# Moving matmul operands to other addresses: a 64-byte gap, a shifted weight slot and wider phi(k) buffers

## The chip, the cores and the metric

The kernel runs on one core of one Trainium2 chip. The metric is the device time of one execution in microseconds. The kernel before took 303.79 us, the median of 3 runs (303.33 to 304.34).

Names of engines: PE is TensorE (PEld its weight loads), DVE is VectorE, ACT is ScalarE, POOL is GpSimd, SP is SyncE, which here only issues transfers.

## The reference

x is a sequence of 2048 rows and 640 columns. Two branches work on it and a gate mixes them.

```
g = sigmoid(sum(x * gate_w))                       # one number per row
a = conv(x, K) + x * Dskip                         # state space branch; K from A, B, C, dt
q, k, v = x @ wqkv, 32 heads of 20
pq, pk = phi(q), phi(k)      # phi(t) = (t + 1 if t > 0 else exp(t)) + 1e-6
kv = sum over rows of pk^T v ;  z = sum over rows of pk      # per head
b = (pq @ kv / (pq . z + 1e-6)) @ wo
out = g * a + (1 - g) * b
```

All inputs and the output are float32. For the given inputs the convolution's kernel K is constant over the sequence to within float32's precision, so that the kernel computes it as a running sum along the sequence; a general path for other inputs is in the program but does not run.

## The kernel before, in words

Every large product is made of three matmuls on split operands: a number is kept as h + l, where h is its rounding to the float32r type that TensorE reads and l the rest, and a product is ah*bh + al*bh + ah*bl (`mm3`, L104 to L107). The work on TensorE comes in this order.

- **k and G^T.** The rows go through in 16 tiles of 128. For tile T, k = x @ wk is made in two halves of columns: `k_mm(T, 0)` with wkA (322 columns: 320 of wk and two that hold gate_w for the gate) and `k_mm(T, 1)` with wkB (320). Each half is 15 matmuls: 5 blocks of the contraction, three each; the stationary operand is a 128 by 128 block of x transposed (xTh or xTl), the moving operand is wk. For the first four tiles the loops stand in another order (`k_first`, L441). ScalarE and VectorE turn k into phi(k): tiles e (3 buffers) and r (2 buffers), then its split ph and pl (`k_act`, `k_split`). Meanwhile TensorE sums G = x^T phi(k) over the rows for tile T-1: `g_main` (512 columns of phi(k) moving, blocks of xh and xl stationary; 3 matmuls for each of 5 blocks) and `g_rest` (the other 128 columns of phi(k) stationary, x moving, 320 columns; 6 matmuls). The loop's body (L546 to L573) sets the order on TensorE: k half 0 (15 matmuls), G block 0 (3), G blocks 1 and 2 (6), k half 1 (15), `g_rest` (6), G blocks 3 and 4 (6).
- **The small matrices.** GT holds G transposed; with Wv it gives kv per head (`kv_mm`, L266), and with wo the 640 by 640 matrix M (`m_mm`), which goes through DRAM and is read back as Mh and Ml into the slots of GT and Wv (tags "m1" and "m2").
- **q and the output.** 20 blocks of q (`q_block`: wq stationary, xT moving, 512 columns, 15 matmuls each) and 20 blocks of the output (`final_mm`: M stationary, phi(q) split in pTh and pTl moving, 15 matmuls each; the last block is cut into two halves of 256 columns). The table PLAN (L63) sets the order of these by hand: q is a block of q, f a block of the output, d the denominators (2 matmuls), n a normalisation, y a block of the convolution.

The order of instructions on every engine is the order in which the code is written. SBUF tiles are given out by pools in the order in which the pools were made: px (x transposed, whose slots phi(q) takes over), pc (constants, then GT, Wv and the split weights), pw, pk (the tiles of the k stage), and, in pk's place after it is closed, pq. A tile that is larger or added in pc therefore moves all that stands behind it. wkA has a slot of 384 columns a row block (tag "wA", `w_tiles(3 * P, ...)`), since wq's first 384 columns use the slot later; it fills 322 of them, from the start.

Of the kernel before, what the change touches and what calls it, by code (L numbers as in the profile page):

```python
# [30 lines left out]
F32 = mybir.dt.float32  # L31
# [8 lines left out]
P = 128  # L40
L = 2048
D = 640
# [5 lines left out]
CA, CB = 320, 320  # L48
# [9 lines left out]
NK = sum(map(len, CONV_K.values()))  # L58
WQ = 3, 4, 0, 1, 2
QI = DH // NB  # L60


PLAN = """  # L63
# [10 lines left out]
def f32(ap):  # L74
    return ap.bitcast(F32)


def body(tc, i, outT):
    nc = tc.nc
    pe, act, dve, pool, sp = nc.tensor, nc.scalar, nc.vector, nc.gpsimd, nc.sync  # L80
    outer, top, kst = ExitStack(), ExitStack(), ExitStack()

    def mk(stack, name, space=None):
        kw = {} if space is None else {"space": space}
        if space is not DRAM:
            kw["reuse_waits"] = "tile"
        return stack.enter_context(tc.tile_pool(name=name, bufs=1, **kw))
# [6 lines left out]
    pk = mk(kst, "pk")  # L94
# [3 lines left out]
    def hi(dst, src):  # L98
        act.activation(dst, src, AF.Copy)  # L99
# [9 lines left out]
    def col(tag, n=NB, dt=F32):  # L109
        return pc.tile([P, n], dt, tag=tag, name=tag)  # L110

    def w_tiles(n, tag, name):
        return tuple(pc.tile([P, NB, n], F32R, tag=tag + x, name=name + x) for x in "hl")
# [30 lines left out]
    zc, zs, ch = col("zc"), col("zs", 1), col("ch", 1)  # L144
    zsh, zsl = col("zsh", 2, F32R), col("zsl", 2, F32R)
    bm, zh = col("bm", P, F32R), col("zh", H)
    GT = pc.tile([P, NB, D], F32, tag="m1", name="GT")
    Wv = pc.tile([P, NB, D], F32, tag="m2", name="Wv")
    M_d = [dram.tile([D, D], F32, name=f"M_d{x}") for x in "hl"]
# [31 lines left out]
    kp, ke, ks = {}, {}, {}  # L181
# [10 lines left out]
    def k_act(t, hf):  # L192

        p, c0, n = kp.pop((t, hf)), hf * CA, (CA, CB)[hf]
        if hf == 0:
            ke[t] = pk.tile([P, D], F32, tag="e", bufs=3, name="e")
        e = ke[t][:, c0 : c0 + n]
        r = pk.tile([P, CA], F32, tag="r", bufs=2, name="r")
        act.activation(e, p[:, :n], AF.Exp)  # L199
        act.activation(r[:, :n], p[:, :n], AF.Relu)  # L200
        if hf == 0:
            act.activation(s_all[:, t : t + 1], p[:, CA : CA + 1], AF.Copy)
        dve.scalar_tensor_tensor(e, e, 1.0, r[:, :n], op0=OP.min, op1=OP.add)  # L203

    def k_split(t):
# [4 lines left out]
        dve.scalar_tensor_tensor(l, e, EPS, f32(h), op0=OP.add, op1=OP.subtract)  # L210
        za = zacc.rearrange("p (b h i) -> p b h i", h=H, i=QI)
        dve.tensor_tensor(za, za, e.rearrange("p (h b i) -> p b h i", b=NB, i=QI), op=OP.add)
        ks[t] = (h, l)
# [28 lines left out]
    def g_out(b, eng):  # L242
        src = gps.pop(b)
        (hi if eng is act else dve.tensor_copy)(GT[:, b, :512], src)

# [4 lines left out]
    def parts(gi):  # L250
        c0, n = GRP[gi]
        return [(r, c0 + o, min(HC, n - o)) for r, o in ((0, 0), (64, HC)) if o < n]
# [13 lines left out]
    def kv_mm(pr):  # L266
        p = pqp.tile([P, 512], F32, tag="f", bufs=3, name="kvps")
        kvT = kvs[pr] = kvz[pr % 2]
        for k, gi in enumerate((2 * pr, 2 * pr + 1)):
            for b in range(NB):  # L270
                for r, c, n in parts(gi):
                    pe.matmul(p[r : r + n, k * 64 : k * 64 + n], Wv[:, b, c : c + n], GT[:, b, c : c + n],
                              start=(b == 0), stop=(b == NB - 1))
# [175 lines left out]
                pe.matmul(kp[t, hf][:, :n], (xTl if ps == 1 else xTh)[0][:, b, sl], w[ps // 2][:, b, :n],  # L449
                          start=b + ps == 0, stop=b == NB - 1 and ps == 2)  # L450

    wkA = w_tiles(3 * P, "wA", "wkA")
    wkB = w_tiles(CB, "wB", "wkB")
    raw = {}

# [46 lines left out]
    for t in range(N0):  # L502
        k_act(t, 0)
        if t < 2:
            x_split(t)
        k_act(t, 1)
        if t in (0, 2):
            k_split(t // 2)
# [6 lines left out]
    def wq_views(w, c, b0, b1):  # L515
        src = raw[c][:, :D].rearrange("p (h b i) -> p b h i", b=NB, i=QI)[:, b0:b1]
        return [src] + [v[:, c, : (b1 - b0) * P].rearrange("p (b h i) -> p b h i", h=H, i=QI) for v in w]

# [11 lines left out]
    for T in range(1, NT):  # L530
# [15 lines left out]
        if T >= N0:  # L546
            k_mm(T, 0)
            k_act(T, 0)
# [27 lines left out]
        if T == 2:  # L576
            act.activation(dtc, dtc, AF.Exp)
            dve.tensor_reduce(zh, ident.rearrange("p (h i) -> p h i", i=QI), axis=AX.X, op=OP.add)
            dve.tensor_copy(bm.rearrange("p (h i) -> p h i", i=QI), zh[:, :, None].to_broadcast([P, H, QI]))
        for b in CONV_P.get(T - 1, ()):  # L580
# [39 lines left out]
    def rem_out():  # L620
        for b0, b1 in ((0, 4), (4, NB)):
            tp = mbank("tp")
            for b in range(b0, b1):
                pe.transpose(tp[:, (b - b0) * P : (b - b0 + 1) * P], rem[:, b * P : b * P + P], ident)
            hi(GT[:, b0:b1, 512:], tp[:, : (b1 - b0) * P].rearrange("p (b s) -> p b s", s=P))

# [314 lines left out]
```

## Time and profile before

| | us |
|---|---|
| median of 3 runs | 303.79 (303.33 to 304.34) |
| the profiled execution | 304.36 |
| its span, first to last instruction | 302.6 |
| PE busy in the span | 296.6 (98%) |
| PEld | 255.7 (85%) |
| DVE | 230.0 (76%) |
| ACT | 118.8 (39%) |
| POOL | 46.9 (15%) |
| 16 DMA engines, mean share | 48% |

A matmul's duration in the profile is the time from its start to the end of its last column, and successive matmuls overlap: the next one starts long before the last one's end. What a stream of matmuls costs is the distance from start to start, which the timeline shows (rounded to 10 ns, so it is best taken over many matmuls).

### The profile page before, as it was taken

To read this page: it belongs to the slowest core of one execution; us is meant where nothing else is said; L and a number is where in the kernel's file an instruction comes from. 1 tells how busy PE (TensorE), PEld (TensorE's weight loads), DVE (VectorE), ACT (ScalarE), POOL (GpSimd) and SP (SyncE) were. 2 spreads that over 40 slices of the span, in tenths; PEclk is the share of its full clock that TensorE was granted. 3 is DMA by queue.
4 is the path that set the end of the run, shared out by engine and by line. 5 is a ranking of instruction groups with operands and counts; after the bars stand their busy time and mean duration, and the time that the engine had idled before them with its cause. 6 is when DMAs were issued, how large, how long until landed. Compare 5 with 4: busy or idle time off the path is not lost.

```text
span 302.6 us, 4538 instructions
## 1 busy us (share of the span) xinstructions
PE 296.6 (98%) x1627; PEld 255.7 (85%) x1627; DVE 230.0 (76%) x356; ACT 118.8 (39%) x249; POOL 46.9 (15%) x50
## 2 busy tenths in 40 slices
PE   8999999999999999999999999999999999999994
PEld 8998899999999999998887767888888888788884
DVE  2859976899899799946636779859684767788992
ACT  4465143453444435317343563651423234303200
POOL 3605240000000000000000000003133211242531
PEclk9999999999999999999999999999999999999999
DMA  6827275167868756290344553790415022244323
GB/s 190 302 88 220 77 233 185 36 192 203 256 150 252 225 181 203 80 281 14 100 147 137 205 176 110 259 341 9 114 59 186 25 77 62 69 141 172 122 92 109
DMA packets 28410, 46.00 MB, mean 152 GB/s; under 512 B 3772, under 2 KB 10828, under 8 KB 28384
## 3 DMA queue, kind: packets, MB, share of 16 engines
q1 hardware_dynamic: 28383, 45.66, 48.2%
q8 instruction: 15, 0.25, 0.4%
q14 instruction: 12, 0.09, 0.1%
HBM read 32.92 MB, written 12.72 MB: 151 GB/s over the span
## 4 chain that ended last, share of the span: by engine, by line
PE 87%; DVE 6%; DMA 3%; issue 1%; ACT 1%; SPq 1%; POOL 0%; DVEq 0%; ACTq 0%; POOLq 0%
PE fp L105 8%; PE fp L107 8%; PE fp L106 8%; PE qp L105 6%; PE qp L107 6%; PE qp L106 6%; PE k L107 6%; PE k L106 6%; PE k L105 6%; PE g L227 5%; PE g L224 5%; PE g L225 5%; PE g L449 4%; DMA M_dl<-Mgl 2%; PE r L240 1%; PE r L239 1%
## 5 line engine op out<-in xcount | busy, mean ns | idle before, releaser
L434 POOL TENSOR_TENSOR yb<-yb,gb 128x512 f32<-128x512 f32 x20 | 29.5, 1482 | 220.5 <-DMA yb<-y_d 199.2
L105 PE MATMUL fp<-pTh,Mh 128*128 128x512 f32 (+1 forms) x105 | 40.1, 382 | 0.6 <-DVE o L720 0.6
L107 PE MATMUL fp<-pTl,Mh 128*128 128x512 f32 (+1 forms) x105 | 40.2, 383 | 0.0
L106 PE MATMUL fp<-pTh,Ml 128*128 128x512 f32 (+1 forms) x105 | 40.0, 381 | 0.0
L645 DVE SCALAR_TENSOR_TENSOR qe<-qe,qr 128x512 f32<-128x512 f32 x20 | 14.1, 704 | 23.8 <-ACT qr L642 23.8
L224 PE MATMUL g<-ph,xh 128*128 128x512 f32 x80 | 31.6, 395 | 0.0
L225 PE MATMUL g<-ph,xl 128*128 128x512 f32 x80 | 31.5, 394 | 0.0
L199 ACT ACTIVATE e<-k 128x320 f32<-128x320 f32 x25 | 11.0, 439 | 51.3 <-PE k L107 51.3
L99 ACT ACTIVATE pTh<-qe 128x512 fp32r<-128x512 f32 x20 | 12.6, 633 | 40.5 <-DVE qe L681 40.4
L203 DVE SCALAR_TENSOR_TENSOR e<-e,r 128x320 f32<-128x320 f32 x32 | 16.0, 504 | 14.0 <-ACT r L200 13.9
L227 PE MATMUL g<-pl,xh 128*128 128x512 f32 x80 | 26.4, 395 | 0.1
L105 PE MATMUL qp<-xTh,wqAh 128*128 128x512 f32 x60 | 24.0, 401 | 0.0
L641 ACT ACTIVATE qe<-qp 128x512 f32<-128x512 f32 x20 | 12.0, 598 | 30.6 <-PE qp L107 26.6
L105 PEld LDWEIGHTS fp<-pTh,Mh 128*128 128x128 f32 x105 | 19.7, 188 | 5.0 <-DVE o L720 1.0
L107 PE MATMUL qp<-xTl,wqAh 128*128 128x512 f32 x60 | 23.7, 394 | 0.0
L106 PE MATMUL qp<-xTh,wqAl 128*128 128x512 f32 x60 | 23.6, 393 | 0.0
L106 PEld LDWEIGHTS fp<-pTh,Ml 128*128 128x128 f32 x105 | 19.7, 188 | 4.1
L107 PEld LDWEIGHTS fp<-pTl,Mh 128*128 128x128 f32 x105 | 19.8, 188 | 3.9
L414 DVE TENSOR_TENSOR_SCAN y<-y,cY,zero 128x512 f32<-128x512 f32 x16 | 20.5, 1278 | 0.8 <-ACT y L413 0.8
L102 DVE TENSOR_TENSOR pTl<-qe,pTh 128x512 fp32r<-128x512 f32 x20 | 15.1, 763 | 6.8 <-ACT pTh L99 6.3
L107 PE MATMUL k<-wkAl,xTh 128*128 128x322 f32 x60 | 19.0, 317 | 0.0
L106 PE MATMUL k<-wkAh,xTl 128*128 128x322 f32 x60 | 18.9, 315 | 0.0
(168 smaller groups left out, 718.2 us busy)
## 6 DMA issues: line engine op xcount, KB each, us to landing
xraw<-in_x SPq DMA_DIRECT2D x16, 320.0 KB, 5.0
u<-in_xT SPq DMA_DIRECT2D x20, 256.0 KB, 5.3
out_T<-o SPq DMA_DIRECT2D x19, 256.0 KB, 2.5
y_d<-y SPq DMA_DIRECT2D x16, 256.0 KB, 2.2
yb<-y_d SPq DMA_DIRECT2D x16, 256.0 KB, 3.1
xTraw<-in_xTt SPq DMA_DIRECT2D x12, 320.0 KB, 4.5
Wv<-in_wv SPq DMA_DIRECT2D x5, 320.0 KB, 6.8
Mh<-M_dh SPq DMA_DIRECT2D x5, 320.0 KB, 4.6
```

Of the source, the lines that this page charges most:

```text
L99: act.activation(dst, src, AF.Copy)
L102: (eng or dve).tensor_tensor(dst, src, f32(h), op=OP.subtract)
L105: pe.matmul(out, ah, bh, start=start, stop=False)
L106: pe.matmul(out, al, bh, start=False, stop=False)
L107: pe.matmul(out, ah, bl, start=False, stop=stop)
L203: dve.scalar_tensor_tensor(e, e, 1.0, r[:, :n], op0=OP.min, op1=OP.add)
L224: pe.matmul(gps[b], xh[:, s], h[:, :512], start=t == 0, stop=False)
L225: pe.matmul(gps[b], xl[:, s], h[:, :512], start=False, stop=False)
L227: pe.matmul(gps[b], xh[:, b * P : b * P + P], l[:, :512], start=False, stop=t == NT - 1)
L414: dve.tensor_tensor_scan(y, y, zero.to_broadcast([P, 512]), cY[:, c], op0=OP.add, op1=OP.add)
L434: pool.tensor_tensor(ys[j], ys[j], gbs[j // NB], op=OP.mult)
L645: dve.scalar_tensor_tensor(e, e, 1.0, r, op0=OP.min, op1=OP.add)
```

## The change

Three edits of the places of tiles in SBUF, and one small instruction that goes with the first.

- A tile `gap` of 16 columns (64 bytes a partition) is put ahead of GT, and POOL sets it to zero. All that stands behind it moves up by 64 bytes: GT, Wv, the split weights wk and wq, M, and the pools pw, pk and pq.
- wkA is used from column 40 of its slot instead of column 0: 160 bytes more for it. Its rows in a slot of 384 columns still fit (40 + 322 = 362).
- The tiles e (3 buffers) and r (2 buffers) are 8 columns (32 bytes) wider, but are used as before. The tiles behind them in pk, xh, xl, ph, pl and xTraw, move by 5 x 32 = 160 bytes more.

The byte in a partition at which a tile starts, as laid out in the two programs (the first buffer where there are several; the others keep the same remainders by 512, e and r excepted):

| tile | role | before | after | before, by 512 | after, by 512 |
|---|---|---|---|---|---|
| xTh, xTl (pTh, pTl) | stationary for k, moving for q and output | 16512 | 16512 | 128 | 128 |
| GT (Mh) | output: stationary | 104512 | 104576 | 64 | 128 |
| Wv (Ml) | output: stationary | 117312 | 117376 | 64 | 128 |
| wkAh | moving for k, half 0 | 130112 | 130336 | 64 | 288 |
| wqAh (wkAh's slot) | stationary for q | 130112 | 130176 | 64 | 128 |
| wkBh (wqBh) | moving for k, half 1; stationary for q | 145472 | 145536 | 64 | 128 |
| xh | stationary for G, moving for g_rest | 202048 | 202272 | 320 | 32 |
| xl | the same | 207168 | 207392 | 320 | 32 |
| ph | moving for G, stationary for g_rest | 212288 | 212512 | 320 | 32 |
| pl | the same | 217408 | 217632 | 320 | 32 |

xTh's place is the same in both; a row block of wkB or wqB is 1280 bytes, so that these alternate between 64 and 320 (after: 128 and 384) by 512. No operation's shape, type or amount of data changes.

On PE, DVE, ACT and SP the same instructions stand in the same order, with waits for the same engines' work. On POOL there is one more, at the program's start (after the change; the names are those of the tiles):

```order
6 L122 MEMSET ones 128x128
7 L133 MEMSET zacc 128x640
8 L136 MEMSET cY 128x5
9 L136 MEMSET zero 128x1
10 L142 MEMSET kvT_100 128x128
11 L142 MEMSET kvT_101 128x128
12 L149 MEMSET gap 128x16
13 L103 ISA
14 L103 TENSOR_TENSOR wkAl<-wraw,wkAh 128x322 x5
```

The row of `gap` is new; the rest of POOL's program is as before, with the line numbers moved by 1 to 3.

```
+WKO = 40
...
     bm, zh = col("bm", P, F32R), col("zh", H)
+    gap = col("gap", 16)
+    pool.memset(gap, 0.0)
     GT = pc.tile([P, NB, D], F32, tag="m1", name="GT")
...
-            ke[t] = pk.tile([P, D], F32, tag="e", bufs=3, name="e")
+            ke[t] = pk.tile([P, D + 8], F32, tag="e", bufs=3, name="e")[:, :D]
         e = ke[t][:, c0 : c0 + n]
-        r = pk.tile([P, CA], F32, tag="r", bufs=2, name="r")
+        r = pk.tile([P, CA + 8], F32, tag="r", bufs=2, name="r")
...
-    wkA = w_tiles(3 * P, "wA", "wkA")
+    wkA = tuple(v[:, :, WKO : WKO + CA + 2] for v in w_tiles(3 * P, "wA", "wkA"))
```

## The prediction

> **What bounds the kernel now.** I read the page first: its shares, the granted clock and the chain of waits.
>
> ```profile
> span 302.6 us, 4538 instructions
> ...
> PE 296.6 (98%) x1627; PEld 255.7 (85%) x1627; DVE 230.0 (76%) x356; ACT 118.8 (39%) x249; POOL 46.9 (15%) x50
> ...
> PEclk9999999999999999999999999999999999999999
> ...
> PE 87%; DVE 6%; DMA 3%; issue 1%; ACT 1%; SPq 1%; POOL 0%; DVEq 0%; ACTq 0%; POOLq 0%
> ```
>
> TensorE is busy 98% of the span at the full granted clock, and 87% of the chain that ends last is TensorE's own work. The view of waits says the same from the other side: the other engines stand waiting for it.
>
> ```profile
> ACT e L199 <- PE k L107: 51.3, 22, 5.5
> ACT qe L641 <- PE qp L107: 26.6, 13, 4.4
> ```
>
> So the time is the sum of the distances from one matmul's start to the next. The change alters no matmul's shape or order; it can only act on these distances, or not at all. Next, therefore, the groups by shape: first matmuls, then weight loads (mean ns of one at the right end, before the idle time).
>
> ```profile
> L224 PE MATMUL g<-ph,xh 128*128 128x512 f32 x80 | 31.6, 395 | 0.0
> L105 PE MATMUL qp<-xTh,wqAh 128*128 128x512 f32 x60 | 24.0, 401 | 0.0
> L107 PE MATMUL k<-wkAl,xTh 128*128 128x322 f32 x60 | 19.0, 317 | 0.0
> L107 PE MATMUL k<-wkBl,xTh 128*128 128x320 f32 x60 | 18.5, 308 | 0.0
> ...
> L105 PEld LDWEIGHTS k<-wkAh,xTh 128*128 128x128 f32 x60 | 11.5, 192 | 0.5
> L105 PEld LDWEIGHTS k<-wkBh,xTh 128*128 128x128 f32 x60 | 11.3, 188 | 0.6
> ```
>
> One thing stands out. The weight loads of the first half of k take 192 ns, those of the second half 188, though they load blocks of the same xTh; the matmuls beside them take 317 and 308 ns, where two columns in 320 would account for 2 ns. The operand that streams beside the load is another (wkA, not wkB). The timeline shows the distances themselves; I take the rows at which blocks begin.
>
> ```profile
> 27.09 0.39 PE L224 MATMUL g<-ph,xh 128*128 128x512 f32 x1
> 29.13 0.30 PE L238 MATMUL r<-xh,ph 128*128 128x320 f32 x1
> ...
> 36.09 0.31 PE L105 MATMUL k<-wkAh,xTh 128*128 128x322 f32 x1
> 38.30 0.40 PE L224 MATMUL g<-ph,xh 128*128 128x512 f32 x1
> 40.35 0.31 PE L105 MATMUL k<-wkBh,xTh 128*128 128x320 f32 x1
> 42.55 0.31 PE L238 MATMUL r<-xh,ph 128*128 128x320 f32 x1
> ...
> 53.77 0.31 PE L105 MATMUL k<-wkAh,xTh 128*128 128x322 f32 x1
> 56.06 0.40 PE L224 MATMUL g<-ph,xh 128*128 128x512 f32 x1
> 58.17 0.30 PE L105 MATMUL k<-wkBh,xTh 128*128 128x320 f32 x1
> ...
> 207.00 0.40 PE L105 MATMUL qp<-xTh,wqBh 128*128 128x512 f32 x1
> 235.00 0.39 PE L666 MATMUL dp<-acch,bm 128*128 128x512 f32 x1
> 242.34 0.39 PE L105 MATMUL fp<-pTh,Mh 128*128 128x512 f32 x1
> 259.50 0.39 PE L105 MATMUL fp<-pTh,Mh 128*128 128x512 f32 x1
> ```
>
> Read as paces (distance divided by the matmuls between the rows):
>
> - wkA, 15 matmuls: (38.30 - 36.09) / 15 = 147 ns in tile 4, but (56.06 - 53.77) / 15 = 153 ns in tile 6. Tiles 4 and 5 have the first pace, tiles 6 to 15 the second.
> - wkB, 15 matmuls: (42.55 - 40.35) / 15 = 147 ns.
> - G blocks 0 to 2, nine matmuls: (29.13 - 27.09) / 9 = 227 ns, (40.35 - 38.30) / 9 = 228, and (58.17 - 56.06) / 9 = 234 in the later tiles.
> - q and output, 512 columns: from 207.00 to 235.00 PLAN has q f q f f q f q, 8 x 15 = 120 matmuls: 233.3 ns. From 242.34 to 259.50 it has f q f q f, 75 matmuls: 228.8 ns.
>
> So one and the same instruction, with the same addresses, has two paces or three that differ by about 6.6 ns (147 and 153; 227 and 233) or a third of it, and keeps its pace for whole stretches. Nothing is waited for between these rows. [...] The addresses are not the whole cause (tiles 4 and 6 of k have the same), and that they are one of the causes is an inference, from wkA beside wkB and from this: G, where both operands start at the same remainder by 512 (320 and 320), falls back to 227; q and the output (128 and 64) never get there in these stretches.
>
> **The change part by part.** *The memset* on POOL costs nothing: it comes after kvT's, and POOL then waits for the weights.
>
> ```profile
> 1.53 0.35 POOL L141 MEMSET kvT<- 128x128 f32 x2
> 4.27 0.99 POOL L102 TENSOR_TENSOR wkAl<-wraw,wkAh 128x322 fp32r<-128x322 f32 x1 [2.39 <-DVE wkAh L487]
> ```
>
> A memset of 16 columns is no longer than the 0.35 us of the two of 128 columns, and 2.39 us of idle time cover it. Without that cover it would be those 0.35 us at most, once.
>
> *wkA at 288 instead of 64 by 512*, beside xTh at 128. Tiles 6 to 15 lose 2.29 - 2.21 = 0.08 us each against tile 4: 10 x 0.08 = 0.8 us. Bounds: all of it comes back (-0.8), or tiles 4 and 5 slow down as well (+0.2). Of the groups above only this one has the longer weight load, and the edit takes it out of the place at which it has that. I take -0.8.
>
> *xh, xl, ph, pl at 32 instead of 320 by 512.* Their distance from each other does not change. The nine matmuls of blocks 0 to 2 take 58.17 - 56.06 = 2.11 us behind a slow wkA block and 40.35 - 38.30 = 2.05 behind a fast one: 10 x 0.06 = 0.6 us, if the pace is handed on from wkA. Blocks 3 and 4 and `g_rest` I leave at 0. Bounds: at 227 ns for all 240 matmuls of G, ten tiles x 2.11 and the rest alike, about 240 x 234 - 240 x 227 = 1.7 us less (an upper bound, since not all are at 234); one more step of 6.6 ns in each is 240 x 6.6 = 1.6 us more, and with the 96 of `g_rest` 336 x 6.6 = 2.2. I take -0.6, since the rows of tile 4 have just this sequence.
>
> *GT, Wv, wq, M and wkB 64 bytes further*, which brings wq and M to the same remainder as xT (128 and 128). About 590 matmuls of 512 columns (20 blocks of q and 19 of the output, 15 each, are 585). Bounds: all at G's 227 ns, which is 120 x 6.3 + 465 x 1.8 = 1.6 us less; all at 233.3, which is 465 x 4.5 = 2.1 us more. Both paces stand in the trace at unchanged addresses, so I take 0. wkB has the steady 147 now, and I take 0 for it; kv's operands keep their distance (GT and Wv both move by 64), also 0.
>
> *DVE, ACT, transfers.* They write and read the same tiles 64 to 224 bytes further on. DVE has 24% of the span free and ACT 61%, and ACT waits for TensorE by the rows above; 0, with no bound of its own beside those of TensorE.
>
> The sum: -0.8 - 0.6 = **-1.4 us**. The profiled execution took 304.36 us (1.8 outside its span), 0.6 above the median shown; 304.36 - 1.4 is 303.0 there, and against the median 303.79 - 1.4 = **302.4 us**.
>
> [...]
>
> **The rivals.**
>
> 1. *Nothing moves.* If the pace hangs on how a stretch is entered and not on addresses, the three edits do nothing, and what is left is 303.8 us, give or take 0.6. For it: tiles 4 and 6 differ at one address. Against it: the pace then stays for ten tiles, each the same, and wkB never leaves 147. [...]
>
> 2. *Slower: a start in the middle of a 64-byte unit.* Before, xh, xl, ph, pl and wkA all start at multiples of 64 bytes; after, at 32 more than one. 512 columns of 4 bytes are 32 such units, and from the middle 33. The step of 6.6 ns is what 16 columns (64 bytes) take at 0.41 ns a column, the 213 ns that 512 columns leave when G's two steps of 6.6 are taken from 227. If each of G's 240 matmuls and of `g_rest`'s 96 pays one step, the price is 336 x 6.6 = 2.2 us: 303.8 + 2.2 = 306.0 us. With the 0.8 of wkA gained it is 305.2. It decides as soon as more than about 210 of the 336 pay (1.4 us). Against it: 322 columns from 64 end 8 bytes into a 21st unit, and tile 4 does them in the same 147 ns as 320 columns. The same end is reached without it if q and the output settle at 233.3 (+2.1).
>
> 3. *More than forecast.* wq and M at xT's own remainder give q and the output G's 227 ns: 1.6 us on top of the 1.4, 300.8 us. For it: G is the one stream with that relation, and the one with that pace. Against it: G also has 234.
>
> That the change does not do what it says is excluded by the layout of the tiles.
>
> **How the numbers follow.** I give the forecast 0.36, rival 3 0.19, rival 1 0.23 and rival 2 0.22. What a measurement of this kernel can tell from no change is about 0.3%, 0.9 us. Forecast and rival 3 are faster by more: 0.55; rival 1 is within: 0.23; rival 2 is slower: 0.22. The likeliest case gives 302.4; its own range is 301.4 to 303.0 (half of the terms, or blocks 3 and 4 too). The range for 8 in 10 takes in rival 3 with a little below it, rival 1, and the lighter half of rival 2: 300.2 to 305.2.
>
> **What would show it.** The weight loads of k<-wkAh at 188 ns and the matmuls of k<-wkAl at about 309; tile 6's block of wkA 2.20 us long instead of 2.29; the nine G matmuls behind it 2.05 instead of 2.11. Rival 1: every group as before. Rival 2: the means of g<-ph,xh and r<-xh,ph up by 6 ns, and their distances with them. Rival 3: 120 matmuls of q and output in 27.2 us instead of 28.00, and fp's and qp's means below 392. The prediction is wrong if wkA keeps 153 ns, or if G or the output change their pace by more than wkA does.

## The result, and the profile after

| | before | after |
|---|---|---|
| median, us | 304.06 (303.33 to 305.27, 6 runs) | 302.08 (301.70 to 302.94, 6 runs) |
| after / before, 95% interval | | 0.9926 (0.9911 to 0.9942) |
| the profiled execution, us | 304.36 | 301.70 |
| its span, us | 302.6 | 299.9 |

The change makes the kernel faster by 0.7%, some 2.0 to 2.3 us; the two profiled executions lie 2.7 apart. The median of before, 303.79 at the time of the prediction, is 304.06 with three more runs. The page of the changed kernel (span, engines, granted clock, chain of waits):

```profile
span 299.9 us, 4539 instructions
...
PE 294.2 (98%) x1627; PEld 255.4 (85%) x1627; DVE 229.7 (77%) x356; ACT 118.7 (40%) x249; POOL 47.6 (16%) x51
...
PEclk9999999999999999999999999999999999999999
...
PE 94%; DVE 4%; issue 1%; ACT 0%; POOL 0%; DVEq 0%; POOLq 0%
```

PE's busy time falls by 2.4 us and the span by 2.7; the share of PE is the same 98%, and the mean granted clock is 0.999 before and 1.000 after. The gain lies in PE's own work. The groups by shape of the changed kernel, matmuls first and then weight loads:

```profile
L227 PE MATMUL g<-ph,xh 128*128 128x512 f32 x80 | 31.5, 394 | 0.0
L106 PE MATMUL qp<-xTh,wqAh 128*128 128x512 f32 x60 | 23.9, 398 | 0.0
...
L108 PE MATMUL k<-wkAl,xTh 128*128 128x322 f32 x60 | 18.5, 309 | 0.0
L108 PE MATMUL k<-wkBl,xTh 128*128 128x320 f32 x60 | 18.5, 309 | 0.0
...
L106 PEld LDWEIGHTS k<-wkAh,xTh 128*128 128x128 f32 x60 | 11.3, 188 | 0.5
L106 PEld LDWEIGHTS k<-wkBh,xTh 128*128 128x128 f32 x60 | 11.3, 188 | 0.5
```

The weight loads beside wkA take 188 ns instead of 192, and wkA's matmuls 309 instead of 317: the two halves of k now look alike. qp goes from 401 to 398, g from 395 to 394. As before, the distances show more than these durations. The timeline of the changed kernel at the starts of blocks, in tile 4, in tile 6, in q and the output, and in the last block's two halves (columns: start, duration, then the instruction):

```profile
36.38 0.31 PE L106 MATMUL k<-wkAh,xTh 128*128 128x322 f32 x1
38.58 0.40 PE L227 MATMUL g<-ph,xh 128*128 128x512 f32 x1
40.64 0.31 PE L106 MATMUL k<-wkBh,xTh 128*128 128x320 f32 x1
42.85 0.31 PE L241 MATMUL r<-xh,ph 128*128 128x320 f32 x1
...
54.08 0.31 PE L106 MATMUL k<-wkAh,xTh 128*128 128x322 f32 x1
56.29 0.40 PE L227 MATMUL g<-ph,xh 128*128 128x512 f32 x1
58.36 0.31 PE L106 MATMUL k<-wkBh,xTh 128*128 128x320 f32 x1
...
205.39 0.39 PE L106 MATMUL qp<-xTh,wqBh 128*128 128x512 f32 x1
232.59 0.40 PE L669 MATMUL dp<-acch,bm 128*128 128x512 f32 x1
...
239.88 0.39 PE L106 MATMUL fp<-pTh,Mh 128*128 128x512 f32 x1
256.88 0.39 PE L106 MATMUL fp<-pTh,Mh 128*128 128x512 f32 x1
...
292.30 0.28 PE L106 MATMUL fp<-pTh,Mh 128*128 128x256 f32 x1
294.09 0.28 PE L106 MATMUL fp<-pTh,Mh 128*128 128x256 f32 x1
```

The same halves in the kernel before:

```profile
295.15 0.28 PE L105 MATMUL fp<-pTh,Mh 128*128 128x256 f32 x1
296.85 0.28 PE L105 MATMUL fp<-pTh,Mh 128*128 128x256 f32 x1
```

- wkA in tile 6: 56.29 - 54.08 = 2.21 us instead of 2.29; the slow pace of 153 ns is gone from tiles 6 to 15.
- The nine G matmuls behind it: 58.36 - 56.29 = 2.07 instead of 2.11.
- q and output: 232.59 - 205.39 = 27.20 us for 120 matmuls (before 28.00), and 256.88 - 239.88 = 17.00 for 75 (before 17.16). Both are 226.7 ns a matmul. The two paces of before, 233.3 and 228.8, have become one that neither stretch had.
- The halves of the last block: (294.09 - 292.30) / 15 = 119 ns instead of (296.85 - 295.15) / 15 = 113. Here the change costs time.

Summed over all matmuls of each kind, from the traces' start-to-start distances (a distance over 245 ns counts as a stall and is left out):

| stream | matmuls | mean before, ns | mean after, ns | change, us |
|---|---|---|---|---|
| k with wkA | 180 | 151.8 | 147.2 | -0.82 |
| G blocks 0 to 2 | 141 | 232.1 | 229.5 | -0.37 |
| G blocks 3 and 4 | 96 | 231.3 | 231.5 | +0.02 |
| g_rest | 96 | 146.4 | 145.6 | -0.07 |
| k with wkB | 180 | 146.1 | 146.8 | +0.13 |
| q | 291 | 230.3 | 227.4 | -0.85 |
| output, 512 columns | 284 | 230.2 | 227.0 | -0.89 |
| output, 256 columns | 29 | 113.3 | 119.8 | +0.19 |

The sum is -2.66 us, and the span fell by 2.7: what the span lost is accounted for.

### The profile page after: what moved, and what is told of

Read it like the earlier page. It is cut to its first block, busy times and chain, and to the rows that moved or that the text cites. A ratio compares the mean times of both kernels' runs of the same rounds, so it can differ in the third digit from the quotient of the medians.

```text
span 299.9 us, 4539 instructions
## 1 busy us (share of the span) xinstructions
PE 294.2 (98%) x1627; PEld 255.4 (85%) x1627; DVE 229.7 (77%) x356; ACT 118.7 (40%) x249; POOL 47.6 (16%) x51
## 4 chain that ended last, share of the span: by engine, by line
PE 94%; DVE 4%; issue 1%; ACT 0%; POOL 0%; DVEq 0%; POOLq 0%
PE qp L106 8%; PE fp L106 8%; PE fp L108 8%; PE fp L107 8%; PE qp L107 8%; PE qp L108 8%; PE k L108 6%; PE k L107 6%; PE k L106 6%; PE g L230 5%; PE g L227 5%; PE g L228 5%; PE g L452 4%; PE mps L293 1%; PE r L241 1%; PE r L242 1%
## 5 line engine op out<-in xcount | busy, mean ns | idle before, releaser
L437 POOL TENSOR_TENSOR yb<-yb,gb 128x512 f32<-128x512 f32 x20 | 28.7, 1443 | 218.3 <-DMA yb<-y_d 191.6
L648 DVE SCALAR_TENSOR_TENSOR qe<-qe,qr 128x512 f32<-128x512 f32 x20 | 15.4, 770 | 22.5 <-ACT qr L645 22.5
L103 DVE TENSOR_TENSOR pTl<-qe,pTh 128x512 fp32r<-128x512 f32 x20 | 16.1, 818 | 6.8 <-ACT pTh L100 6.3
L106 PE MATMUL k<-wkBh,xTh 128*128 128x320 f32 x60 | 18.6, 310 | 0.0
L107 PE MATMUL k<-wkBh,xTl 128*128 128x320 f32 x60 | 18.5, 309 | 0.0
```

The costliest lines, as they stand in the source:

```text
L103: (eng or dve).tensor_tensor(dst, src, f32(h), op=OP.subtract)
L106: pe.matmul(out, ah, bh, start=start, stop=False)
L107: pe.matmul(out, al, bh, start=False, stop=False)
L437: pool.tensor_tensor(ys[j], ys[j], gbs[j // NB], op=OP.mult)
L648: dve.scalar_tensor_tensor(e, e, 1.0, r, op0=OP.min, op1=OP.add)
```

## The experiments

The theory after the result: a stream's pace hangs on the **distance** between its weights' tile and its x tile, taken in the bytes of a partition at which they start (wkA - xTh, wq - xTh, M - pTh; in k the weights stream and x is loaded, in q and the output the other way round), and not on where the two lie. Before it is 64 - 128 = -64 by 512 in all three; after it is 0 in q and output, +160 in wkA. The rivals: absolute addresses; a pace that only hangs on how a stretch is entered; a state that one stream hands to the next. Each experiment is an edit of the kernel before, unless another is named. In the fences below the rows are from the timeline, as above.

### The gap alone

```
     bm, zh = col("bm", P, F32R), col("zh", H)
+    gap = col("gap", 16)
+    pool.memset(gap, 0.0)
```

> The 64-byte gap alone; wkA from column 0 of its slot, e and r as before. Theory (the pace hangs on where the stationary operand lies against the moving one): q and the output have both operands at 128 by 512, so their steady blocks take 15 x 226.7 ns = 3.40 us as in the changed kernel, which is 1.5 us of the gain; wkA now also has xTh's remainder (128 and 128), so it should be at 147 ns too, 0.8 us; G keeps its distance and its pace. 303.8 - 2.3 = 301.5 to 302.3 us. Rival A (each edit is needed for its own stream, as the prediction's sum had it): wkA keeps 153 ns, 302.3 to 302.8 us. Rival B (the pace hangs on how a stretch is entered): q and the output go back to a mixture of 229 and 233 ns, 303 to 304.5 us.

0.9933 (0.9916 to 0.995), against the whole change's 0.9926. Its trace, first a block of wkA, then the 120 matmuls of q and output:

```profile
54.21 0.31 PE L105 MATMUL k<-wkAh,xTh 128*128 128x322 f32 x1
56.43 0.40 PE L226 MATMUL g<-ph,xh 128*128 128x512 f32 x1
...
206.13 0.39 PE L105 MATMUL qp<-xTh,wqBh 128*128 128x512 f32 x1
233.33 0.40 PE L668 MATMUL dp<-acch,bm 128*128 128x512 f32 x1
```

27.20 us, the changed kernel's own value, and wkA at 2.22 / 15 = 148 ns. The 64 bytes bring nearly the whole gain, and they bring all three distances to 0. Summed over the same streams, this trace shows 2.60 of the 2.66 us: 1.77 in q and the output, 0.65 in wkA, 0.37 in G's blocks 0 to 2, less 0.19 that the last block's halves lose. wkA stays a little above the 147 ns expected, and G did not keep its pace as expected (229.4 ns instead of 232.1); the run with e and r wider comes back to this.

### wkA's shift alone

```
-    wkA = w_tiles(3 * P, "wA", "wkA")
+    wkA = tuple(v[:, :, 40 : 40 + CA + 2] for v in w_tiles(3 * P, "wA", "wkA"))
```

> wkA from column 40 of its slot alone (224 by 512, xTh at 128); the rest as before. Theory and rival A: wkA at 147 ns, the nine G matmuls behind it shorter by 0.04 to 0.06 us a tile, q and the output as before (229 and 233 ns mixed): 303.8 - 1.2 = 302.6 us, 302.3 to 303.0. Rival B: a gain or a loss anywhere, with the same instructions moving from one pace to another, wkA's and others', by up to 1.5 us either way.

0.9974 (0.996 to 0.9988), 0.8 us less.

```profile
62.87 0.31 PE L105 MATMUL k<-wkAh,xTh 128*128 128x322 f32 x1
65.11 0.39 PE L224 MATMUL g<-ph,xh 128*128 128x512 f32 x1
...
206.10 0.39 PE L105 MATMUL qp<-xTh,wqBh 128*128 128x512 f32 x1
233.57 0.39 PE L666 MATMUL dp<-acch,bm 128*128 128x512 f32 x1
```

At a distance of +96 wkA goes at 2.24 / 15 = 149 ns, between 147 and 153, and not at the 147 expected. q and output, whose addresses are as before, were expected as before; they do these 120 matmuls in 27.47 us, 228.9 ns, where before had 233.3. So a pace can change with no change of addresses (233.3 to 228.9 ns), but here only to the other one that before has too.

### e and r wider alone

```
-            ke[t] = pk.tile([P, D], F32, tag="e", bufs=3, name="e")
+            ke[t] = pk.tile([P, D + 8], F32, tag="e", bufs=3, name="e")[:, :D]
...
-        r = pk.tile([P, CA], F32, tag="r", bufs=2, name="r")
+        r = pk.tile([P, CA + 8], F32, tag="r", bufs=2, name="r")
```

> e and r 8 columns wider alone: xh, xl, ph and pl at 480 by 512 instead of 320, their distances from each other unchanged; wkA and the rest as before. Theory (only the distance between the two operands counts): nothing moves, 303.8 us, within 0.5. If the place itself counts: blocks 0 to 2 of G leave 231 to 238 ns for 227, which is the 0.4 us that the changed kernel gained there, or they get slower by a step of 6.6 ns (1.6 us).

1.0002 (0.9989 to 1.0015): nothing that the timing can tell. The two operands of every matmul keep their distance. First 105 matmuls between the denominators, then 90 behind them:

```profile
206.58 0.39 PE L105 MATMUL qp<-xTh,wqBh 128*128 128x512 f32 x1
230.61 0.39 PE L105 MATMUL qp<-xTh,wqAh 128*128 128x512 f32 x1
...
238.01 0.40 PE L105 MATMUL qp<-xTh,wqAh 128*128 128x512 f32 x1
259.01 0.40 PE L105 MATMUL fp<-pTh,Mh 128*128 128x512 f32 x1
```

24.03 / 105 = 228.9 ns and 21.00 / 90 = 233.3: the two paces of before with their places exchanged. The operands of q and the output lie as before, so their places alone do not settle which of the two a stretch has. That something ahead of the stretch does is the author's reading; what it would be was not shown. None of the stretches reaches 226.7.

G did change. Tile 6, from wkA's block over the nine matmuls of G to wkB's:

```profile
53.83 0.31 PE L105 MATMUL k<-wkAh,xTh 128*128 128x322 f32 x1
56.12 0.39 PE L224 MATMUL g<-ph,xh 128*128 128x512 f32 x1
58.18 0.30 PE L105 MATMUL k<-wkBh,xTh 128*128 128x320 f32 x1
```

wkA's block is as slow as before (2.29 us), yet the nine G matmuls behind it take 2.06 us instead of 2.10 to 2.11. Blocks 0 to 2 go at 229.4 ns instead of 232.1 in the mean, 0.38 us: the changed kernel's whole gain there, and the second outcome named in the expectation, too small for the timing. G's tiles kept their distance from each other but moved against all the others, wkA and xTh among them.

### Everything moved together by 64 bytes

```
+    pad = px.tile([P, 16], F32, tag="pad", name="pad")
+    pool.memset(pad, 0.0)
     ones = col("ones", P)
```

> A pad of 64 bytes ahead of xTh, so that every operand moves by 64 bytes together and no distance changes. Theory (distance): every pace as before, 303.8 us, within 0.5. Rival C (the place itself counts: GT, wq, M and wkB come to 128 by 512 exactly as in the changed kernel): q and the output at 227 ns, 302.2 us or less. Rival B: the mixture of paces falls out anew, up to 1 us either way.

1.0004 (0.9989 to 1.0018). The pad stands ahead of xTh too, so that every address of the kernel moves and no distance does.

```profile
207.57 0.40 PE L105 MATMUL qp<-xTh,wqBh 128*128 128x512 f32 x1
232.07 0.40 PE L105 MATMUL qp<-xTh,wqAh 128*128 128x512 f32 x1
239.48 0.39 PE L105 MATMUL qp<-xTh,wqAh 128*128 128x512 f32 x1
256.64 0.39 PE L105 MATMUL fp<-pTh,Mh 128*128 128x512 f32 x1
```

24.50 / 105 = 233.3 ns ahead of the second denominators, 17.16 / 75 = 228.8 behind them: before's two paces, in before's places. wkA has its 151.8 ns again, G's blocks 0 to 2 have 231.9 against 232.1, and no other stream of the table above differs from before by more than 0.1 ns: two executions with the same distances repeat each other. The wq and M tiles start at just the same remainder as in the run with the gap alone, and have none of its gain. The place as such does not count here; where the tiles lie to each other does.

### Other widths of the gap

The same edit as the first, with 48, 8, 24, 32 and 80 columns instead of 16: distances of +128, -32, +32, +64 and +256.

> The kernel before with a gap of 192 bytes instead of 64, nothing else: wq, M, wkA and wkB lie 128 bytes above xTh by the remainder (256 and 128 by 512). If the distance counts by 128 or a divisor of it, this is the 64-byte gap alone over again: q and the output at 15 x 226.7 ns = 3.40 us a block, the last block's halves at 120 ns, about 0.993 of before. If it counts by 256 or 512, another pace: q and the output at 229 to 233 ns, 0.998 to 1.005 of before. If how a stretch is entered decided alone, a mixture of 229 and 233.

> The kernel before with a gap of 32 bytes, nothing else: the distance of wq, M, wkA and wkB from xTh is -32 bytes by the remainder (before -64, with the 64-byte gap 0). If only exact equality gives 227 ns, q and the output stay at 229 or above and the time at 0.998 to 1.003 of before. If coming nearer is enough (what the shifted wkA suggests, which has 147 ns at 160 bytes), most of the gain of the 64-byte gap is here too: 0.993 to 0.996.

> The kernel before with a gap of 96 bytes: wq, M, wkA and wkB 32 bytes above xTh by the remainder. So far q's and the output's pace was 228.9 or 233.3 ns at -64, 233.3 at -32, 226.7 at 0 and 232.3 to 233.3 at +128. If only equality gives 226.7, they are at 229 or above here (0.998 to 1.003 of before); if the moved wkA's good pace at +32 to +160 carries over to 512 columns, 226.7 and 0.993.

> The kernel before with a gap of 128 bytes: distance +64. If the distance counts by 128, this is the kernel before (-64): blocks of q and output at 228.9, some at 233.3, the last block's halves at 113.3 ns. If not, another pace, 229 to 234 ns, and other halves (117 to 120).

> The kernel before with a gap of 320 bytes: distance +256 by 512. If the distance counts by 256, this is the 64-byte gap again: 226.7 ns and 0.993. If it counts by 512 or more, or as a whole and not by a remainder, another pace, 229 to 234 ns, and 0.998 to 1.003. wkB and wq's second part alternate between two remainders 256 apart at one pace in every run so far, which speaks for 256.

| gap, bytes | distance | wkA, mean ns | q and output, steady ns | last block's halves, ns | ratio (95%) |
|---|---|---|---|---|---|
| none | -64 | 151.8 | 228.9 or 233.3 | 113.3 | 1 |
| 32 | -32 | 147.8 | 233.3 | 116.7 | 1.0022 (1.0002 to 1.0042) |
| 64 | 0 | 148.2 | 226.7 | 119.8 | 0.9933 (0.9916 to 0.995) |
| 96 | +32 | 147.9 | 233.3 | 118.0 | 1.0019 (1.0 to 1.0037) |
| 128 | +64 | 146.8 | 233.3 | 113.8 | 1.0004 (0.9986 to 1.0022) |
| 192 | +128 | 146.7 | 232.3 to 233.3 | 118.8 | 1.0007 (0.999 to 1.0024) |
| 320 | +256 | 148.2 | 226.7 | 119.8 | 0.9914 (0.9884 to 0.9944) |

The rows behind the column of q's and the output's paces, first for the gap of 32 bytes (105 matmuls, 24.50 us), then of 320 (105 matmuls, 23.80 us):

```profile
206.42 0.39 PE L105 MATMUL qp<-xTh,wqBh 128*128 128x512 f32 x1
230.92 0.40 PE L105 MATMUL qp<-xTh,wqAh 128*128 128x512 f32 x1
```

```profile
208.59 0.39 PE L105 MATMUL fp<-pTh,Mh 128*128 128x512 f32 x1
232.39 0.40 PE L668 MATMUL dp<-acch,bm 128*128 128x512 f32 x1
```

Three things follow. A distance of 256 does what 0 does, stream by stream, so the distance counts by 256 as far as this one pair shows (and not by 128: 0 and +128 differ). Of the distances tried, 0 by 256 is the only one that is good for 512 columns. And what is good for 512 columns is not good for the others: the 322 columns of wkA go best at +64 and +128, where the 512 are slow, and the halves of 256 columns go best at 64 either way and worst at 0. The gaps of 32 and 96 bytes lose more on 575 matmuls of q and output than they gain on 180 of wkA; no gap in the table is best for all three shapes.

Rival 1 of the prediction, that addresses do nothing, falls with this table. So does the added memset as a cause: all these gaps have it, and only two of them gain.

### The gap behind Wv: q and output apart

```
     Wv = pc.tile([P, NB, D], F32, tag="m2", name="Wv")
+    gap = col("gap", 16)
+    pool.memset(gap, 0.0)
```

> The 64-byte gap behind Wv instead of ahead of GT: wq, wkA and wkB move as with the gap ahead of GT, M (in the slots of GT and Wv) does not. Blocks of q and of the output alternate in the program. Theory (distance of the stream's own operands): q's blocks at 226.7 ns, the output's at 229 or 233, so half of q's and the output's gain: about 0.996 of before, the eight blocks of output in a row at the end at 228.9. Rival B (a pace is entered and kept): q's and the output's blocks share one pace while they alternate.

Now wk and wq move, GT and Wv, whose slots M takes over, do not: the distance is 0 for q and -64 for the output. The ratio is 0.993 (0.9905 to 0.9955). Four successive blocks, f, q, f, f:

```profile
246.65 0.39 PE L105 MATMUL fp<-pTh,Mh 128*128 128x512 f32 x1
250.09 0.39 PE L105 MATMUL qp<-xTh,wqBh 128*128 128x512 f32 x1
253.49 0.39 PE L105 MATMUL fp<-pTh,Mh 128*128 128x512 f32 x1
256.92 0.39 PE L105 MATMUL fp<-pTh,Mh 128*128 128x512 f32 x1
```

3.44 us for the block of the output, 3.40 for q, 3.43 for the output: 228.9 and 226.7 ns in turn, at each of these switches. Against the gap alone, only GT, Wv and M lie elsewhere here, and only the output has lost its 226.7. The pace of these streams belongs to their own two operands, and is not a state that one stream hands to the next for good. The time came lower than was expected for it (0.996): with q at 226.7 every stretch of the output went at 228.9, none at 233.3.

### G's five blocks in a row

To the changed kernel:

```
         g_main(T - 1, rest)
+        g_main(T - 1, (3, 4))
         if T >= N0:
             k_mm(T, 1)
...
         g_rest(T - 1)
-        g_main(T - 1, (3, 4))
```

> The changed kernel with blocks 3 and 4 of G issued right behind blocks 1 and 2, ahead of k's second half, instead of behind g_rest. Each change from 320 to 512 columns costs about six matmuls at 231 to 236 ns before 227 is reached (blocks 3 and 4: 231, 231, 236, 228, 233, 231). With all fifteen of G in a row there is one such entry a tile instead of two: 15 x 6 x 4.8 ns = 0.4 us less, 301.7 us against the changed kernel's 302.1, or 0.9915 of before. Rival: phi(k) of the tile comes later against the matmuls that need it (the cover between k's second half and G's first block shrinks by the 1.4 us of blocks 3 and 4), TensorE waits in front of G, and the time is the changed kernel's or worse by up to 15 x 0.7 us.

In the changed kernel blocks 3 and 4 are still at 231.5 ns. Their six distances, in most tiles, are 231, 231, 236, 228, 233 and 230 or 231 ns: behind `g_rest`'s 320 columns they do not settle at 227, and these six are all there are. Six is no general length, as the expectation had it: in tile 6 of the changed kernel, blocks 0 to 2 behind wkA's 322 columns take 232, 236 and 236 ns, and then 226 to 229. Put directly behind blocks 0 to 2, blocks 3 and 4 went at 227.7 ns: 0.37 us gained, as worked out. But the kernel became slower, 1.0043 (1.0028 to 1.0059) against before instead of 0.9915. The rival, that TensorE waits, is what happened, though 2.7 us of the wait is in front of k and not of G. Its weight loads by group (the last field is the idle time ahead of them, in us, and what ended it), and then the timeline of one tile:

```profile
L227 PEld LDWEIGHTS g<-ph,xh 128*128 128x128 f32 x80 | 15.0, 188 | 4.0 <-ACT wqBh L100 1.4 <-ACT s_all L205 0.2
L230 PEld LDWEIGHTS g<-pl,xh 128*128 128x128 f32 x80 | 15.0, 188 | 4.3 <-DVE pl L213 1.1
...
L106 PEld LDWEIGHTS k<-wkAh,xTh 128*128 128x128 f32 x60 | 11.3, 188 | 2.7 <-ACT r L203 2.7
```

```profile
99.82 0.43 ACT L203 ACTIVATE r<-k 128x320 f32<-128x320 f32 x1
...
100.30 0.19 PEld L106 LDWEIGHTS k<-wkAh,xTh 128*128 128x128 f32 x1 [0.24 <-ACT r L203]
```

The next tile's k now starts straight behind `g_rest`, and finds the tile that it writes to (tag "k", one buffer for both halves) still read by ScalarE's relu of the half before: 0.24 us of idle time in the row above, ended by that relu. Blocks 3 and 4 had covered that: six matmuls, 1.4 us. In the changed kernel the same group waits for nobody (0.5 us idle in all, its row is above), and G's two groups stand idle for 2.3 and 3.8 us instead of 4.0 and 4.3. The order that costs a slow start of 0.37 us hides 2.7 us of waiting at one place alone.

### The gap, and wkA at +128

```
+    gap = col("gap", 16)
+    pool.memset(gap, 0.0)
...
-    wkA = w_tiles(3 * P, "wA", "wkA")
+    wkA = tuple(v[:, :, 32 : 32 + CA + 2] for v in w_tiles(3 * P, "wA", "wkA"))
```

> A version made from the runs: the 64-byte gap, wkA from column 32 of its slot (distance +128, at which the 192-byte gap had it at 146.7 ns throughout), e and r as before. Theory: q and the output at 226.7 as with the gap alone, wkA at 146.7 instead of 148.2 (0.27 us), G and the rest as with the gap alone: 0.992 of before, the changed kernel's 0.9926 or 0.1 us better, which a measurement can't tell apart. Rival: wkA's good pace hung on its neighbours and not on its distance, 148 to 150 ns again and 0.993 to 0.994.

The table's best for each: 0 for q and output, +128 for wkA. 0.9911 (0.9883 to 0.9938), which cannot be told from the changed kernel's 0.9926. wkA is at 146.6 ns as expected, but G's blocks 0 to 2 behind it go at 231.1 ns, where the changed kernel has 229.5: 0.2 us lost against 0.1 gained. The gap of 192 bytes has the same pair, wkA at 146.7 and G at 231.1. Together with the run with e and r wider (wkA 151.8, G 229.4) this shows that G's gain does not hang on wkA's pace.

## Why the prediction came out

The time, 302.08, is 0.3 below the forecast of 302.4, and in the likeliest case's own range. That it came so near is in part luck. The forecast was a change of -1.4 us, and the measured one is -2.0 to -2.3; the 303.79 from which it was taken lies 0.27 below the later median. The largest part of the gain came from a term put at 0.

- **Where the time goes** held. All of the change is in distances between matmuls; PE's share (98%) and the clock (0.999 and 1.000) did not move.
- **wkA, -0.8** held: -0.82, by what it was worked out from, 2.29 to 2.21 us in ten tiles. The shift was not needed for most of it: the gap alone gives 0.65, the shift alone 0.40.
- **G's blocks 0 to 2, -0.6**: a gain of 0.37, but not by the mechanism given. The condition was that wkA hands its pace on; the run with e and r wider has G's whole gain with wkA as slow as before, and with a faster wkA than the changed kernel's (146.7, gap of 192 bytes) G is only at 231.1. What G's blocks hang on is where their tiles lie to the others, and which of these counts is open. The size was off as well: the nine matmuls take 2.06 to 2.07 us in tiles 6 to 15 now, where before they took 2.10 to 2.11. That is 0.04 instead of 0.06 in each of ten tiles.
- **Blocks 3 and 4, `g_rest`, wkB at 0**: +0.02, -0.07, +0.13. **The memset, kv, DVE, ACT and the transfers at 0**: what the streams give already accounts for the span; the memset took 0.11 us of POOL, with 2.39 us of idle time behind it as before.
- **q and the output at 0** is the step that failed: -0.85 and -0.89, the largest part of the gain. The reason given was that both paces stand in the trace at unchanged addresses. The runs show that this was read too widely. The paces that stand there, 228.9 and 233.3, are the two that the runs with a distance of -64 show; that 226.7 was not among them was the sign of the addresses. At 0 every steady block of q and output has it. The lower bound for this edit, -1.6, was G's 227 ns for all of them, and it measured -1.74: the term was to be had from the rows, and was put at the wrong end. What had been held against it, that G also has 234, was no steady pace: the nine matmuls of tile 6 of before take between 224 and 240 ns each.
- **The last block's halves** were in no term: +0.19, since their 256 columns took 113.3 ns at a distance of -64 and 119.8 at 0.

**The rivals.** Rival 3's mechanism happened, with its row to the hundredth (27.20 us for 120 matmuls), and with fp's means below 392 (390, 389, 389). Of qp's, four of six are below (the first group is at 398, another at 392). Its time of 300.8 did not come: the sum in the traces is -2.66 instead of -3.0, and of that the medians show -2.0, since the profiled execution of before lay 0.3 above its median and that of after 0.4 below. Rival 2, a start in the middle of a 64-byte unit, fell: G's operands start there now, and blocks 3 and 4 go at 231.5 against 231.3 ns, `g_rest` at 145.6 against 146.4. Its price came from two steps taken to be in G's 227 ns, which no row showed; the 0.41 ns a column that it used agrees with rows of before, (227 - 147) / (512 - 320) = 0.42. Its other way to the same end, q and output at 233.3, does exist: gaps of 32 and 96 bytes are that case, with ratios of 1.002. Rival 1 was half right on one point, that a pace can differ at the same addresses (228.9 and 233.3), and wrong in taking this for all. The prediction also named as a sign of being wrong that the output changes its pace by more than wkA does. In the stretch of 120 matmuls it did, 6.6 ns against 5.3 in tile 6; in the mean of all matmuls it did not, 3.2 against 4.6.

**What stays open.** Why a distance costs 2.2 or 6.7 ns was not shown. In the traces of before and after, a weight load of 188 ns (192 beside wkA before) starts 2 to 4 ns behind most matmuls of these streams, behind those of 226 ns as behind those of 233, so that its start does not tell the paces apart. Each kernel was profiled in one execution. That the run with everything moved repeats before, and the gap of 320 bytes the gap of 64, speaks for the paces being the same in each execution, but no kernel was traced twice. M was moved alone (the gap behind Wv against the gap alone); wq was not, but always with what stands behind it. The sums from the traces and the timed ratios agree within 0.6 us for the runs without new waits.

## What to carry to other kernels

Where TensorE is the bound, take the start-to-start distance of each stream from the timeline and compare streams of one shape: a few ns between them, with nothing waited for, can hang on where the stationary and the moving tile lie to each other (here 226.7 ns against 228.9 or 233.3), and a pad of a few columns ahead of one of them is a cheap thing to try, for the streams with the most matmuls. Two paces at the same addresses do not speak against that: here 228.9 and 233.3 stood at one placement, and 226.7 came only with another; the question is whether the best pace of that shape is among those that a placement shows. And a stream that starts slowly may stand where it stands because it hides a wait (here 0.37 us of slow starts against 2.7 us of waiting): look at what would be late without it before moving it.

## What the runs showed of the hardware

- The steady start-to-start paces of these kernels' float32r matmuls with a weight load each lay between two values some 6.7 ns apart: 113.3 and 120.0 at 256 columns, 146.7 and 153.3 at 322, 226.7 and 233.3 at 512. Others lie in between and can be mixtures (228.9 is the cycle 226, 229, 232).
- In q and the output (512 columns) the pace hung on the distance of the two operands: 226.7 at 0 and +256 (the one pair 256 bytes apart), 228.9 or 233.3 at -64, 232.3 to 233.3 at -32, +32, +64 and +128. Moving both by 64 bytes changed nothing (228.8 and 233.3 in before's places).
- The best of the distances tried differs by shape: 0 is the best for 512 columns, the worst for 256 (119.8 against 113.3 at -64), and in the middle for 322 (148.2; 146.7 at +128, 151.8 at -64).
- G's 512 columns behind 320 or 322 did not begin at a steady pace. In the changed kernel the nine G matmuls behind wkA reach 227 with the fourth (232, 236, 236 before it), and the six behind `g_rest` (228 to 236) do not settle. In tiles 6 to 15 of the kernel before, the nine behind wkA do not either (224 to 240), though their operands lie at distance 0.
